# A cheaper VectorE exponential, a shorter rsqrt chain and an earlier preparation of heads in an attention kernel with normalized queries and keys

## Chip, cores and metric

One core of one Trainium2 chip. The metric is the device time of one execution in microseconds (us), the median of the runs. All runs quoted are of the state "fast". Engines: PE is TensorE (PEld its weight loads), DVE is VectorE, ACT is ScalarE, POOL is GpSimd, SP (SPq its queue) is SyncE, which here does nothing but issue DMAs, in a fixed order. In the views of the profile L402 is line 402 of that kernel, `p_ring<-psA` means that `psA` is read and `p_ring` written, and "issue" stands for idle time for which the profile shows no cause.

## The reference

32 heads, 2048 tokens, 20 numbers per head and token (B=1). Each query and key is divided by its norm, the logits are scaled by one `t` per head, softmax, then the product with V:

```python
qn = q / (jnp.sqrt((q * q).sum(axis=-1, keepdims=True)) + eps)
kn = k / (jnp.sqrt((k * k).sum(axis=-1, keepdims=True)) + eps)
logits = jnp.einsum('bhqd,bhkd->bhqk', qn, kn) * t[None, :, None, None]
attn = _softmax(logits, axis=-1)
return jnp.einsum('bhqk,bhkd->bhqd', attn, v)
```

With heads of only 20, the matrix products are small. The 32 x 2048 x 2048 exponentials are the work, and they are shared between two engines.

## The kernel before

A small scheduler in the kernel takes all tasks with planned durations and priorities ("due", in units of heads) and fixes, once, the order in which each engine does them. Every engine then runs its list in order and waits for semaphores. **An engine can thus be held up by the head of its list although a later task could run.**

The keys of a head are 16 chunks of 128, and one chunk is four units of 512 queries. ScalarE takes most chunks: TensorE writes QK products into `psA`, ScalarE takes the exponential of three units at a time into `p_ring`, TensorE multiplies that with V into `psO`. VectorE takes 3, 3, 3, 4 chunks of four successive heads, with an exponential made of integer operations: a 16-bit integer that is linear in the logit is, read as fp16, roughly 2 to that power, and two products with its mantissa correct the error.

```python
DVE_TILES = [4 if h % 4 == 3 else 3 for h in range(H)]
[...]
# one VectorE chunk: four evictions (t1), two integer passes (r, m), two fp16 products (T, U)
t1 = ... eng.tensor_scalar(xt[s][:, 512*g:512*g+512], psD[:, :], X_MUL, X_ADD, ALU.mult, ALU.add)
tr_ = ... eng.tensor_single_scalar(rr[s], xt[s], 0x3FF, ALU.bitwise_xor)
tm  = ... eng.tensor_scalar(mm[s2], xt[s], 0x3FF, 0x3C00, ALU.bitwise_and, ALU.bitwise_or)
tT  = ... eng.tensor_tensor(tt[s2], xt[s].bitcast(FP16), mm[s2].bitcast(FP16), ALU.mult)
tU  = ... eng.tensor_tensor(uu[s], tt[s2], mm[s2].bitcast(FP16), ALU.mult)
# the exponential is the sum of three terms, made by three products with V, two of them on scaled V
pS = pv("S", xt[s], v8, t1s); pR = pv("R", rr[s], v2, [tr_]); pU = pv("U", uu[s], vaug, [tU])
```

(shortened). Before its first QK product a head must be prepared:

```python
def add_prep(h):
    due = h - 1.6                    # planned 1.6 heads before the head is due
    # SyncE: loads of q (4), k, v
    # VectorE: squares, sums, 11 small steps of a reciprocal square root, normalize into qkn
    # SyncE: one transpose qkT<-qkn, four copies qz<-qkT, six copies kR<-qkT
```

The first QK product of a head waits for the last of those ten copies. `psD` is a single PSUM bank in which the QK products of VectorE's chunks go by, one unit at a time.

## Time and profile before

859.52 us (two runs, 858.82 and 860.21). The page of the profiled execution, its first part (busy time and share of the span):

```profile
span 855.5 us, 12498 instructions
## 1 busy us (share of the span) xinstructions
PE 706.3 (83%) x4836; PEld 201.5 (24%) x4928; DVE 783.2 (92%) x1380; ACT 749.7 (88%) x546; POOL 52.9 (6%) x79
```

No engine is alone at its limit. The groups of instructions (busy us, mean ns of one | idle time of the engine just before them, and what ended it):

```profile
L402 ACT ACTIVATE p_ring<-psA 128x1536 bf16<-128x1536 f32 x544 | 748.2, 1463 | 100.4 <-PE psA L342 84.2 <-remote 6.0 <-PE psO L351 4.4
...
L430 DVE TENSOR_SCALAR xt<-psD 128x512 int16<-128x512 f32 x416 | 284.1, 683 | 55.2 <-PE psD L342 50.1 <-remote 1.1 <-PE psO L351 1.0
...
L443 DVE TENSOR_TENSOR uu<-tt,mm 128x2048 f16<-128x2048 f16 x104 | 126.6, 1217 | 0.0
...
L437 DVE TENSOR_SCALAR mm<-xt 128x2048 int16<-128x2048 int16 x104 | 71.3, 685 | 0.0
```

ScalarE did nothing for 100.4 us of the span. Some 28 us of this is the start, as the list of waits shows (total us, times, longest):

```profile
ACT p_ring L402 <- PE psA L342: 84.2, 68, 28.3
...
DVE xt L430 <- PE psD L342: 50.1, 56, 6.4
PE psA L342 <- DMA kR<-qkT: 45.5, 8, 29.4
...
PE psD L342 <- DMA kR<-qkT: 10.1, 6, 3.0
```

To find what the rest is, take its longest stop, at 571 us. ScalarE's timeline (start, duration, and in brackets the idle time before):

```profile
560.96 1.45 ACT L402 ACTIVATE p_ring<-psA 128x1536 bf16<-128x1536 f32 x1 [0.21 <-PE psA L342]
570.63 2.79 ACT L402 ACTIVATE p_ring<-psA 128x1536 bf16<-128x1536 f32 x2 [8.22 <-PE psA L342]
574.61 1.45 ACT L402 ACTIVATE p_ring<-psA 128x1536 bf16<-128x1536 f32 x1 [1.19 <-PE psD L342]
576.78 1.45 ACT L402 ACTIVATE p_ring<-psA 128x1536 bf16<-128x1536 f32 x1 [0.72 <-PE psA L342]
```

The same stop in TensorE's timeline. It had waited for a kR copy:

```profile
569.45 0.60 PE L342 MATMUL psA<-qz,kR 64*128 64x512 bf16 x1 [4.64 <-DMA kR<-qkT]
...
569.99 1.69 PE L342 MATMUL psA<-qz,kR 128*128 128x512 bf16 x4
571.47 0.63 PE L342 MATMUL psD<-qz,kR 128*128 128x512 bf16 x1
```

And in SyncE's, the copies of that head, issued behind a transpose, which itself came when the head had been normalized, at 556.8:

```profile
556.84 1.27 SPq L315 DMA_TRANSPOSE qkT<-qkn  x1
558.15 2.69 SPq L268 DMA_DIRECT2D qk_sb<-in_q_dram  x4
560.89 0.62 SPq L271 DMA_DIRECT2D qk_sb<-in_k_dram  x1
561.57 2.48 SPq L321 DMA_DIRECT2D qz<-qkT  x4
564.09 3.77 SPq L327 DMA_DIRECT2D kR<-qkT  x6
```

Ten copies at 0.6 us each and the loads of another head lie between transpose and first product; with 2.1 us for the last copy to land, that makes 569.4, when TensorE goes on. This is a **late head**. ScalarE's gaps after the stop are 1.19 and 0.72 us, not the usual 0.2. The slices of the page (clock granted to TensorE, tenths of full speed, 40 slices):

```profile
PEclk9999999999999999899997999979999899999799
```

Busy time by stretches of 100 us (busy us and count per engine; then the granted clock):

```profile
core 0: us, PE busy (x) PEld busy (x) DVE busy (x) ACT busy (x) POOL busy (x), PEclk, DMA share, GB/s
500.00:600.00 100.00, 81.79 (x541) 22.77 (x550) 89.88 (x162) 84.13 (x62) 7.11 (x8) 0.91 0.24 40
700.00:800.00 100.00, 87.19 (x621) 25.15 (x632) 97.69 (x173) 94.89 (x71) 5.19 (x6) 0.99 0.21 40
```

### The profile page before, as it was taken

Reading aid. Unit: us, or ns where it says so; the run is one execution under the profiler, and the core shown is the slowest. Engines: PE = TensorE matmul, PEld = TensorE weight load, DVE = VectorE, ACT = ScalarE, POOL = GpSimd, SP = SyncE. Lnnn points to the kernel's source line nnn. Section 1 sums busy time; section 2 is a strip of 40 time slices with the busy share of each in tenths; the row PEclk is TensorE's granted clock in tenths of the full one; section 3 lists DMA queues with packets and bytes.
Section 4 is the critical chain, followed back from the end, with each engine's and each line's share of the span. In section 5 each row is a group of like instructions: output and inputs, shape, how many; then the busy total and the mean of one; then the engine's idle time right before and its main releaser. Section 6 shows DMA issues by size and latency. Waiting matters only on the chain.

```text
span 855.5 us, 12498 instructions
## 1 busy us (share of the span) xinstructions
PE 706.3 (83%) x4836; PEld 201.5 (24%) x4928; DVE 783.2 (92%) x1380; ACT 749.7 (88%) x546; POOL 52.9 (6%) x79
## 2 busy tenths in 40 slices
PE   0598998989887988788986998959988798898887
PEld 0122222222222222122221222212222122222122
DVE  7699998989998999799987999879998899999798
ACT  0599999989999899799986999859998799999797
POOL 3000000001000000000000101000000000000000
PEclk9999999999999999899997999979999899999799
DMA  6441203331213330413314213042121421220200
GB/s 54 89 65 30 49 10 53 53 52 23 47 38 54 53 53 5 67 35 53 47 14 67 54 32 53 8 77 44 31 44 18 80 34 37 45 41 22 66 1 8
DMA packets 198346, 36.49 MB, mean 43 GB/s; under 512 B 173712, under 2 KB 198288, under 8 KB 198288
## 3 DMA queue, kind: packets, MB, share of 16 engines
q1 hardware_dynamic: 198288, 35.70, 25.4%
q8 instruction: 38, 0.62, 0.3%
q14 instruction: 20, 0.16, 0.1%
HBM read 7.87 MB, written 2.62 MB: 12 GB/s over the span
## 4 chain that ended last, share of the span: by engine, by line
DVE 51%; PE 26%; SPq 13%; DMA 4%; issue 3%; ACT 2%
DVE xt L430 19%; PE psA L342 12%; DVE tt L440 9%; PE psO L351 8%; DVE uu L443 8%; PE psD L342 6%; SPq L327 5%; SPq L321 4%; DVE mm L437 3%; SPq L268 3%; DMA kR<-qkT 3%; DVE rr L435 3%; ACT p_ring L402 2%; DVE qkn L310 2%; DVE oT L360 2%
## 5 line engine op out<-in xcount | busy, mean ns | idle before, releaser
L402 ACT ACTIVATE p_ring<-psA 128x1536 bf16<-128x1536 f32 x544 | 748.2, 1463 | 100.4 <-PE psA L342 84.2
L342 PE MATMUL psA<-qz,kR 64*128 64x512 bf16 (+1 forms) x1169 | 316.1, 401 | 61.5 <-DMA kR<-qkT 43.7
L430 DVE TENSOR_SCALAR xt<-psD 128x512 int16<-128x512 f32 x416 | 284.1, 683 | 55.2 <-PE psD L342 50.1
L351 PE MATMUL psO<-p_ring,vaug 128*32 128x512 bf16 x1632 | 165.6, 396 | 8.4 <-issue 5.3
L342 PEld LDWEIGHTS psA<-qz,kR 64*128 64x128 bf16 (+1 forms) x1224 | 85.1, 94 | 267.9 <-issue 163.7
L342 PE MATMUL psD<-qz,kR 128*128 128x512 bf16 x296 | 119.2, 403 | 34.4 <-DVE xt L430 15.7
L342 PE MATMUL psA<-qz,qkT 64*128 64x512 bf16 (+1 forms) x395 | 133.3, 400 | 5.3 <-DMA kR<-qkT 1.8
L443 DVE TENSOR_TENSOR uu<-tt,mm 128x2048 f16<-128x2048 f16 x104 | 126.6, 1217 | 0.0
L440 DVE TENSOR_TENSOR tt<-xt,mm 128x2048 f16<-128x2048 f16 x104 | 126.5, 1216 | 0.1
L435 DVE TENSOR_SCALAR rr<-xt 128x2048 int16<-128x2048 int16 x104 | 71.4, 686 | 0.2
L437 DVE TENSOR_SCALAR mm<-xt 128x2048 int16<-128x2048 int16 x104 | 71.3, 685 | 0.0
L351 PEld LDWEIGHTS psO<-p_ring,vaug 128*32 128x32 bf16 x1632 | 42.0, 93 | 110.7 <-issue 100.9
L279 POOL TENSOR_SCALAR v<-vaug 128x128 bf16<-128x128 bf16 x32 | 21.7, 677 | 701.8 <-DMA vaug<-in_v_dram 701.8
L351 PE MATMUL psO<-uu,vaug 128*32 128x512 f16 x416 | 41.8, 392 | 19.8 <-DVE uu L443 18.7
L342 PEld LDWEIGHTS psD<-qz,kR 128*128 128x128 bf16 x312 | 30.3, 97 | 96.3 <-DVE xt L430 57.7
L342 PEld LDWEIGHTS psA<-qz,qkT 64*128 64x128 bf16 (+1 forms) x408 | 32.6, 94 | 68.6 <-issue 51.7
L351 PE MATMUL psO<-xt,v 128*32 128x512 f16 x416 | 41.4, 388 | 8.1 <-DVE oT L360 5.8
L342 PE MATMUL psD<-qz,qkT 128*128 128x512 bf16 x96 | 38.4, 400 | 6.5 <-DVE xt L430 4.7
L351 PE MATMUL psO<-rr,v 128*32 128x512 f16 x416 | 41.2, 386 | 1.5 <-DVE rr L435 1.1
L286 DVE TENSOR_TENSOR sq<-qk_sb 128x640 f32<-128x640 bf16 x32 | 26.2, 819 | 3.4 <-DMA qk_sb<-in_k_dram 3.2
L280 POOL TENSOR_SCALAR v<-vaug 128x128 bf16<-128x128 bf16 x32 | 27.4, 856 | 2.0
L360 DVE STREAM_TRANSPOSE oT<-psO 128x512 f32<-128x512 f32 x32 | 22.7, 710 | 5.2 <-PE psO L351 4.9
(29 smaller groups left out, 190.9 us busy)
## 6 DMA issues: line engine op xcount, KB each, us to landing
kR<-qkT SPq DMA_DIRECT2D x64, 96.0 KB, 2.1
qz<-qkT SPq DMA_DIRECT2D x128, 32.0 KB, 1.9
kR<-qkT SPq DMA_DIRECT2D x64, 64.0 KB, 2.0
qk_sb<-in_q_dram SPq DMA_DIRECT2D x128, 20.0 KB, 2.5
qk_sb<-in_k_dram SPq DMA_DIRECT2D x32, 80.0 KB, 2.5
vaug<-in_v_dram SPq DMA_DIRECT2D x32, 80.0 KB, 3.2
out_dram<-o_stage SPq DMA_DIRECT2D x32, 80.0 KB, 1.9
kR<-qkT SPq DMA_DIRECT2D x64, 32.0 KB, 1.9
```

The source lines that it names most:

```text
L280: return eng.tensor_scalar(v8[b][:, :, :], vaug[b][:, R - VD:R, :], 8.0, None, ALU.mult)
L321: rot[h].append(add("SP", f"qz{h}", lambda eng, tk, g=g: eng.dma_start(qz[bt][32 * g:32 * g + 32, g, :], qkT[bt][32 * g:32 * g + 32, 0:512 ...
L327: rot[h].append(add("SP", f"rot{h}", lambda eng, tk, d0=d0, s0=s0, m=m, dl=dl: eng.dma_start(kR[bt][d0:d0 + m, dl - 1, :], qkT[bt][s0:s0 + ...
L342: return eng.matmul(dst, lhsT, qz[bt][ps, g, :], tile_position=(p0, 0))
L351: last = eng.matmul(psO[32 * g:32 * g + 32, :], lhsT, rhs_of(g), start=start, stop=False, skip_group_check=True, tile_position=(0, 32 * g))
L360: tr = add("DVE", f"tr{h}", lambda eng, tk: eng.transpose(oT[:, :, :].rearrange("p r d -> p (r d)"), psO[:, :]), 0.62, pv_users[h] + ([fin ...
L402: act[w] = add("ACT", f"exp{w}", lambda eng, tk: eng.activation(p_ring[:, p0 * 512:p0 * 512 + n], psA[:, slot * WAVE * 512:slot * WAVE * 5 ...
L430: t1 = add("DVE", f"t1.{j}.{g}", lambda eng, tk, g=g: eng.tensor_scalar(xt[s][:, 512 * g:512 * g + 512], psD[:, :], X_MUL, X_ADD, ALU.mult ...
L435: tr_ = add("DVE", f"r{j}", lambda eng, tk: eng.tensor_single_scalar(rr[s][:, :], xt[s][:, :], 0x3FF, ALU.bitwise_xor), 0.60, t1s + old.ge ...
L437: tm = add("DVE", f"m{j}", lambda eng, tk: eng.tensor_scalar(mm[s2][:, :], xt[s][:, :], 0x3FF, 0x3C00, ALU.bitwise_and, ALU.bitwise_or), 0.60,
L440: tT = add("DVE", f"T{j}", lambda eng, tk: eng.tensor_tensor(tt[s2][:, :], xt[s][:, :].bitcast(FP16), mm[s2][:, :].bitcast(FP16), ALU.mult ...
L443: tU = add("DVE", f"U{j}", lambda eng, tk: eng.tensor_tensor(uu[s][:, :], tt[s2][:, :], mm[s2][:, :].bitcast(FP16), ALU.mult), 1.13, [tT] ...
```

## The change

The intent: less VectorE work per chunk (one fp16 product in place of two, three integer passes in place of two; all three terms on unscaled V, so GpSimd's scaling of V goes), more chunks for VectorE (3, 4, 3, 4: 112 of 512 in place of 104), a shorter rsqrt chain, and heads prepared earlier. The core of the diff, cuts marked:

```diff
-KEXP = 12.9958
+KEXP = 0.63116
+KE_BITS = 6
+SHIFT = 288
 [...]
-X_ADD = 1024.0 * (15.0 - math.log2(KEXP))
+X_ADD = 1024.0 * (15.0 + math.log2(KEXP))
 [...]
-        allt = sorted(self.tasks, key=lambda t: (t.start, t.seq))
+        allt = sorted(self.tasks, key=lambda t: (t.start, pos[t.seq]))
 [...]
-    DVE_TILES = [4 if h % 4 == 3 else 3 for h in range(H)]
+    DVE_TILES = [4 if h % 2 else 3 for h in range(H)]
 [...]
-            due = h - 1.6
+            due = h - 2.2
 [...]
-            vsc[h] = add("POOL", f"vsc{h}", vscale, 0.8, [ld_v[h]] + z_v[b], due)
 [...]
-            c.append(dv("rs", lambda eng, tk: eng.tensor_single_scalar(
-                rs["u"][:, :].bitcast(I32), rs["sum"][:, :].bitcast(I32), 1, ALU.logical_shift_right), 0.12, [c[-1]]))
             c.append(dv("rs", lambda eng, tk: eng.tensor_scalar(
-                rs["u"][:, :].bitcast(I32), rs["u"][:, :].bitcast(I32), 1597463007, -1, ALU.subtract, ALU.mult),
+                rs["u"][:, :].bitcast(I32), rs["sum"][:, :].bitcast(I32), -0.5, 1597463007.0, ALU.mult, ALU.add),
 [...]  (two Newton steps; the first of their instructions, a = y * y, stays)
-                c.append(dv("rs", lambda eng, tk: eng.tensor_tensor(
-                    rs["b"][:, :], rs["a"][:, :], rs["sum"][:, :], ALU.mult), 0.12, [c[-1]]))
-                c.append(dv("rs", lambda eng, tk: eng.tensor_scalar(
-                    rs["c"][:, :], rs["b"][:, :], -0.5, 1.5, ALU.mult, ALU.add), 0.12, [c[-1]]))
-                [...]
-                    tgt[:, :], cur[:, :], rs["c"][:, :], ALU.mult), 0.12, [c[-1]]))
+                c.append(dv("rs", lambda eng, tk: eng.scalar_tensor_tensor(
+                    rs["b"][:, :], rs["a"][:, :], -0.5, rs["sum"][:, :], ALU.mult, ALU.mult), 0.12, [c[-1]]))
+                c.append(dv("rs", lambda eng, tk, cur=cur, tgt=tgt: eng.scalar_tensor_tensor(
+                    tgt[:, :], rs["b"][:, :], 1.5, cur[:, :], ALU.add, ALU.mult), 0.12, [c[-1]]))
 [...]
-            qk = add("PE", f"qkA{w}", f_qk, 0.22 * (len(us) - 1), deps, due_a(us[0]) - 100)
+            qk = add("PE", f"qkA{w}", f_qk, 0.22 * max(1, len(us) - 1), deps, due_a(us[0]) - 100)
 [...]
-                rr[s][:, :], xt[s][:, :], 0x3FF, ALU.bitwise_xor), 0.60, t1s + old.get("r", []), due)
+                ee[s][:, :], xt[s][:, :], 0x7C00, KE_BITS, ALU.bitwise_and, ALU.bitwise_or), 0.60,
+                t1s + old.get("e", []), due)
+            t5 = add(SH_ENG, f"s{j}", lambda eng, tk: eng.tensor_scalar(
+                ss[s][:, :], xt[s][:, :], float(SHIFT - 4096), None, ALU.add), SH_DUR, t1s + old.get("s", []), due)
 [...]
-                mm[s2][:, :], xt[s][:, :], 0x3FF, 0x3C00, ALU.bitwise_and, ALU.bitwise_or), 0.60,
+                mm[s2][:, :], xt[s][:, :], 0x3FF, 0x3800, ALU.bitwise_and, ALU.bitwise_or), 0.60,
 [...]
-            tU = add("DVE", f"U{j}", lambda eng, tk: eng.tensor_tensor(
-                uu[s][:, :], tt[s2][:, :], mm[s2][:, :].bitcast(FP16), ALU.mult), 1.13,
-                [tT] + old.get("u", []), due)
 [...]
-            pS = pv("S", xt[s], v8[b][:, rv, :], t1s)
-            pR = pv("R", rr[s], v2[b][:, rv, :], [tr_])
-            pU = pv("U", uu[s], vaug[b][:, r, :], [tU])
+            pE, pS, pT = pv("E", ee[s], te), pv("S", ss[s], t5), pv("T", tt[s], tT)
```

The chain has 8 steps in place of 11. The two small lines (sort key, `max(1, ...)`) are there for correctness: with 112 chunks ScalarE's units no longer divide by three, the last wave has one unit and a planned duration of zero. A build of the kernel before with only the new chunk counts was found by the race check to let TensorE write a bank of `psA` that ScalarE still read; it was never run.

More of the change, by code (lines that the diff above doesn't have):

```diff
@@ L176, in bass_standalone__qk_norm__prompt_kernel @@
     NX = 3
-    DVE_TILES = [4 if h % 4 == 3 else 3 for h in range(H)]
+    DVE_TILES = [4 if h % 2 else 3 for h in range(H)]
     PE_GROUP = 0.27
-    VD = 4
+    SH_ENG, SH_DUR = "DVE", 0.60
     with ExitStack() as es:
@@ L188, in bass_standalone__qk_norm__prompt_kernel @@
         vaug = [sbuf(f"vaug{i}", [128, R, 32], BF16) for i in range(NB)]
-        v2 = [sbuf(f"v2{i}", [128, VD, 32], BF16) for i in range(NB)]
-        v8 = [sbuf(f"v8{i}", [128, VD, 32], BF16) for i in range(NB)]
         sq = sbuf("sq", [128, 2 * R, D], F32)
-        rs = {x: sbuf(f"rs_{x}", [128, 2 * R], F32) for x in ("sum", "u", "a", "b", "c", "y", "r")}
+        rs = {x: sbuf(f"rs_{x}", [128, 2 * R], F32) for x in ("sum", "u", "a", "b", "y", "r")}
         qkn = [sbuf(f"qkn{i}", [128, 2 * R, 32], BF16) for i in range(2)]
@@ L198, in bass_standalone__qk_norm__prompt_kernel @@
         xt = [sbuf(f"xt{i}", [128, 2048], I16) for i in range(NX)]
-        rr = [sbuf(f"rr{i}", [128, 2048], I16) for i in range(NX)]
+        ee = [sbuf(f"ee{i}", [128, 2048], I16) for i in range(NX)]
+        ss = [sbuf(f"ss{i}", [128, 2048], I16) for i in range(NX)]
         mm = [sbuf(f"mm{i}", [128, 2048], I16) for i in range(2)]
-        tt = [sbuf(f"tt{i}", [128, 2048], FP16) for i in range(2)]
-        uu = [sbuf(f"uu{i}", [128, 2048], FP16) for i in range(NX)]
+        tt = [sbuf(f"tt{i}", [128, 2048], FP16) for i in range(NX)]
         oT = sbuf("oT", [128, R, 32], F32)
@@ L246, in due_a @@
             return h + (i - a0[h]) / nA_head[h]
-        ld_qk, ld_v, norm, trn, rot, vsc = {}, {}, {}, {}, {}, {}
+        ld_v, norm, trn, rot = {}, {}, {}, {}
         qk_users = {h: [] for h in range(H)}
         pv_users = {h: [] for h in range(H)}
-        vs_users = {h: [] for h in range(H)}
         def bc(ap2d, n):
@@ L273, in add_prep @@
             src_v = v[0, h].rearrange("(p r) d -> p r d", p=128)
-            warv = (pv_users[h - NB] + vs_users[h - NB] + [vsc[h - NB]]) if h >= NB else z_v[b]
+            warv = pv_users[h - NB] if h >= NB else z_v[b]
             ld_v[h] = add("SP", f"ldv{h}", lambda eng, tk: eng.dma_start(vaug[b][:, :, 0:D], src_v),
                           0.6, warv, due - 0.4, lat=3.0, dma=f"v{b}")
-            def vscale(eng, tk):
-                eng.tensor_scalar(v2[b][:, :, :], vaug[b][:, R - VD:R, :], 2.0, None, ALU.mult)
-                return eng.tensor_scalar(v8[b][:, :, :], vaug[b][:, R - VD:R, :], 8.0, None, ALU.mult)
-            vsc[h] = add("POOL", f"vsc{h}", vscale, 0.8, [ld_v[h]] + z_v[b], due)
             def dv(name, fn, dur, deps):
@@ L289, in add_prep @@
                         0.75, [c[-1]]))
-            c.append(dv("rs", lambda eng, tk: eng.tensor_single_scalar(
-                rs["u"][:, :].bitcast(I32), rs["sum"][:, :].bitcast(I32), 1, ALU.logical_shift_right), 0.12, [c[-1]]))
             c.append(dv("rs", lambda eng, tk: eng.tensor_scalar(
-                rs["u"][:, :].bitcast(I32), rs["u"][:, :].bitcast(I32), 1597463007, -1, ALU.subtract, ALU.mult),
+                rs["u"][:, :].bitcast(I32), rs["sum"][:, :].bitcast(I32), -0.5, 1597463007.0, ALU.mult, ALU.add),
                 0.12, [c[-1]]))
             cur = rs["u"]
-            for it in range(2):
+            for tgt in (rs["y"], rs["r"]):
                 c.append(dv("rs", lambda eng, tk, cur=cur: eng.tensor_tensor(
                     rs["a"][:, :], cur[:, :], cur[:, :], ALU.mult), 0.12, [c[-1]]))
-                c.append(dv("rs", lambda eng, tk: eng.tensor_tensor(
-                    rs["b"][:, :], rs["a"][:, :], rs["sum"][:, :], ALU.mult), 0.12, [c[-1]]))
-                c.append(dv("rs", lambda eng, tk: eng.tensor_scalar(
-                    rs["c"][:, :], rs["b"][:, :], -0.5, 1.5, ALU.mult, ALU.add), 0.12, [c[-1]]))
-                tgt = rs["r"] if it == 1 else rs["y"]
-                c.append(dv("rs", lambda eng, tk, cur=cur, tgt=tgt: eng.tensor_tensor(
-                    tgt[:, :], cur[:, :], rs["c"][:, :], ALU.mult), 0.12, [c[-1]]))
-                cur = rs["y"]
+                c.append(dv("rs", lambda eng, tk: eng.scalar_tensor_tensor(
+                    rs["b"][:, :], rs["a"][:, :], -0.5, rs["sum"][:, :], ALU.mult, ALU.mult), 0.12, [c[-1]]))
+                c.append(dv("rs", lambda eng, tk, cur=cur, tgt=tgt: eng.scalar_tensor_tensor(
+                    tgt[:, :], rs["b"][:, :], 1.5, cur[:, :], ALU.add, ALU.mult), 0.12, [c[-1]]))
+                cur = tgt
             c.append(dv("rs", lambda eng, tk: eng.tensor_scalar(
@@ L434, in add_dtile @@
                 t1s.append(t1)
-            tr_ = add("DVE", f"r{j}", lambda eng, tk: eng.tensor_single_scalar(
-                rr[s][:, :], xt[s][:, :], 0x3FF, ALU.bitwise_xor), 0.60, t1s + old.get("r", []), due)
+            te = add("DVE", f"e{j}", lambda eng, tk: eng.tensor_scalar(
+                ee[s][:, :], xt[s][:, :], 0x7C00, KE_BITS, ALU.bitwise_and, ALU.bitwise_or), 0.60,
+                t1s + old.get("e", []), due)
+            t5 = add(SH_ENG, f"s{j}", lambda eng, tk: eng.tensor_scalar(
+                ss[s][:, :], xt[s][:, :], float(SHIFT - 4096), None, ALU.add), SH_DUR, t1s + old.get("s", []), due)
@@ L437, in add_dtile @@
             tm = add("DVE", f"m{j}", lambda eng, tk: eng.tensor_scalar(
-                mm[s2][:, :], xt[s][:, :], 0x3FF, 0x3C00, ALU.bitwise_and, ALU.bitwise_or), 0.60,
+                mm[s2][:, :], xt[s][:, :], 0x3FF, 0x3800, ALU.bitwise_and, ALU.bitwise_or), 0.60,
                 t1s + old2.get("m", []), due)
             tT = add("DVE", f"T{j}", lambda eng, tk: eng.tensor_tensor(
-                tt[s2][:, :], xt[s][:, :].bitcast(FP16), mm[s2][:, :].bitcast(FP16), ALU.mult), 1.13,
-                [tm] + old2.get("t", []), due)
@@ L443, in add_dtile @@
-            tU = add("DVE", f"U{j}", lambda eng, tk: eng.tensor_tensor(
-                uu[s][:, :], tt[s2][:, :], mm[s2][:, :].bitcast(FP16), ALU.mult), 1.13,
-                [tT] + old.get("u", []), due)
-            b = h % NB
-            rv = r - (R - VD)
-            base = [vsc[h]] + ([trO[h - 1]] if h else [])
-            def pv(nm, tile, wt, deps):
+                tt[s][:, :], xt[s][:, :].bitcast(FP16), mm[s2][:, :].bitcast(FP16), ALU.mult), 1.13,
+                [tm] + old.get("t", []), due)
@@ L451, in pv @@
+            wt = vaug[h % NB][:, r, :]
+            base = [ld_v[h]] + z_v[h % NB] + ([trO[h - 1]] if h else [])
+            def pv(nm, tile, dep):
                 p = add("PE", f"pv{nm}{j}", lambda eng, tk: pv_mm(
-                    eng, h, wt, lambda g: tile[:, 512 * g:512 * g + 512].bitcast(FP16)), PE_GROUP, deps + base, due + 0.2)
+                    eng, h, wt, lambda g: tile[:, 512 * g:512 * g + 512].bitcast(FP16)), PE_GROUP, [dep] + base,
+                    due + 0.2)
                 pv_users[h].append(p)
@@ L454, in pv @@
                 return p
-            pS = pv("S", xt[s], v8[b][:, rv, :], t1s)
-            pR = pv("R", rr[s], v2[b][:, rv, :], [tr_])
-            pU = pv("U", uu[s], vaug[b][:, r, :], [tU])
-            vs_users[h] += [pS, pR, pU]
-            x_users[j] = {"x": [tr_, tm, tT, pS], "r": [pR], "m": [tT, tU], "t": [tU], "u": [pU]}
+            pE, pS, pT = pv("E", ee[s], te), pv("S", ss[s], t5), pv("T", tt[s], tT)
+            x_users[j] = {"x": [te, t5, tm, tT], "e": [pE], "s": [pS], "m": [tT], "t": [pT]}
```

## The prediction

> **What bounds it now.** Page, part 1: VectorE is busy 783.2 us (92%), ScalarE 749.7 (88%), TensorE 706.3 (83%) of 855.5. No engine alone is the limit: after a start of 30 us (the first exponential starts at 30.6), VectorE and ScalarE are both about 93% busy by windows, and stop together when a head is late. In the list of waits ScalarE waits 84 us for QK products, 28.3 of it the start; the rest is some 15 stops of 1 to 8 us (279, 358, 462, 571, 676 us ...) with slow restarts, and many gaps of 0.2 to 0.4. In the chain of waits these stops end with kR<-qkT DMAs and the SyncE queue (13% of the chain, start included). At 571 us: the rsqrt links of that load lay scattered between large VectorE instructions, it was normalized at 556, and transpose plus 15 DMA issues of 0.6 us brought it at 569.4, too late. From 700 to 800 us, where almost no head is late, VectorE is 97.7% and ScalarE 94.9% busy, with 71 exponential instructions and 14 VectorE chunks, against 62 and 12 from 500 to 600.
>
> **What the change does** (start-to-start times in the timeline, as neighbours overlap).
> - VectorE chunk: four evictions (0.60), two integer passes (0.60), two products (1.13) = 5.9 us; after: four, three, one = 5.3. The Trainium skill ("VectorE: DVE Perf Modes", the perf-mode tier table) gives tensor_scalar on 16-bit SBUF data four results a cycle, tensor_tensor two; the durations of 686 and 1217 ns here agree. The new int16 add should cost 0.60 too. Chunks 104 to 112: 610 to 597 us.
> - rsqrt chain 11 links to 8, each 0.1 us interleaved, 0.22 back to back: -10 us of work; and 3 to 5 us sooner per head, where one link is done per 1 to 2 us. VectorE in all: about 760.
> - ScalarE: 544 to 534 instructions of 1.375 us: 735.
> - TensorE: 8 more VectorE chunks, about +10 us.
> - GpSimd's scaling of V (49 us) goes; it was off the path.
> - Normalization 0.6 head (15 us) sooner: the longest stop is 8 us, so nearly all late heads should vanish. This is the largest part: of 72 us of ScalarE waiting after the start, about 45 belong to such stops.
> - 3,4,3,4 chunks leave VectorE and ScalarE near 23 to 24 us per head on average.
>
> **Sum.** 859.5 - 14 (ScalarE work) - 35 to 45 (stops) = 800 to 810. Cross-check (estimate): 30 start + 735/0.95 + 4 end = 808. TensorE, 716 us of work, was at most 90.6% busy (30 to 100 us); at that rate 825. I predict 810 us, range 793 to 834. Chances: faster by over 2% 0.94, within 2% 0.05, slower 0.01.
>
> **To check after.** VectorE busy 750 to 770 us, ScalarE 735, its waits for QK 45 to 60 instead of 84; TensorE's waits for kR beyond the start below 5 (now 16); the int16 add 0.68 to 0.69 us; stops of several us gone; first exponential 1 to 2 us sooner.
>
> **What would make it wrong.** The int16 add at two a cycle (+0.5 us x 112); the earlier preparation held up by in-order SyncE waits (stores wait 112 us there) or buffers, so that heads are still late (then 835 to 845); TensorE becoming the limit, since three 0.6 us passes give a QK round trip through the single psD bank less cover than two and two 1.13 us products did.

## The result

783.2 us (782.79 and 783.62), ratio 0.9112, 95% interval 0.9073 to 0.9151. A ratio here and below is the mean time of one kernel's fast runs over that of the kernel before in the same rounds, so it is not quite the ratio of the medians. The direction was right; the time lies below the range of 793 to 834.

The page after, first part:

```profile
span 781.0 us, 12650 instructions
## 1 busy us (share of the span) xinstructions
PE 716.0 (92%) x4992; PEld 202.2 (26%) x4992; DVE 750.5 (96%) x1348; ACT 734.1 (94%) x536; POOL 3.8 (0%) x15
```

Groups of instructions:

```profile
L392 ACT ACTIVATE p_ring<-psA 128x1536 bf16<-128x1536 f32 x534 | 732.6, 1458 | 42.0 <-PE psA L332 35.5
...
L420 DVE TENSOR_SCALAR xt<-psD 128x512 int16<-128x512 f32 x448 | 307.0, 685 | 11.7 <-PE psD L332 8.4
...
L433 DVE TENSOR_TENSOR tt<-xt,mm 128x2048 f16<-128x2048 f16 x112 | 136.3, 1217 | 0.0
...
L428 DVE TENSOR_SCALAR ss<-xt 128x2048 int16<-128x2048 int16 x112 | 76.8, 686 | 0.0
```

List of waits; of the 35.5 us, 27.2 are the start, and no kR wait but the first is left:

```profile
ACT p_ring L392 <- PE psA L332: 35.5, 26, 27.2
PE psA L332 <- DMA kR<-qkT: 28.3, 1, 28.3
...
DVE xt L420 <- PE psD L332: 8.4, 27, 0.9
```

Granted clock in slices, and one stretch:

```profile
PEclk9999999999999999999999999999999999999999
```

```profile
core 0: us, PE busy (x) PEld busy (x) DVE busy (x) ACT busy (x) POOL busy (x), PEclk, DMA share, GB/s
500.00:600.00 100.00, 96.39 (x669) 27.46 (x669) 99.05 (x179) 98.50 (x73) 0.00 (x0) 1.00 0.30 48
```

VectorE and ScalarE are now both at 98 to 99%, and TensorE at 96%. Two neighbours in TensorE's timeline, to compare with the 0.6 us matmuls after the stop above; they last 0.4 us:

```profile
560.08 0.40 PE L341 MATMUL psO<-p_ring,vaug 128*32 128x512 bf16 x4
560.41 0.39 PE L332 MATMUL psD<-qz,kR 128*128 128x512 bf16 x1
```

**Where the time came from.** ScalarE's record can be summed without a rest: time to its first exponential, busy time of the exponentials, waiting between them, time from its last exponential to the end (worked out from the two traces, us):

```
          to the first   busy   waiting (in gaps >= 1 us)   to the end    sum
before        30.6      748.2      72.1  (48.1)                4.7        855.6
after         29.5      732.6      14.8  ( 2.5)                4.1        781.0
difference    -1.1      -15.6     -57.3                       -0.6        -74.6
```

Three quarters of the gain are waiting that is gone; the exponentials that moved to VectorE are a fifth.

Two more quantities from the traces, used for all runs below. *Late heads*: of heads 4 to 31, those for whose first QK product TensorE's list came to the wait for the head's last kR copy before that copy had landed, or less than 0.3 us after (landings as the trace assigns them). Before: 16 of 28, after: 0 of 28, with 4.6 to 28.5 us to spare (median 8.4). From normalization to landing it is 14 us in both. Of the 48.1 us of stops before, 47.0 lie between 6 us before and 12 us after the landing of a late head, which is 35% of the time. *Half clock*: time between ScalarE's first and last exponential in which TensorE's granted clock was 0.5. Before: 64.9 us, in ten stretches, each a multiple of 3.4 us, each beside a TensorE gap of 1.4 to 4.6 us; after: none. (Two such gaps, at 189 and 244 us, brought no half clock.) Of ScalarE's 72.1 us of waiting before, 31.8 lie inside those stretches, 8.7 of them while TensorE stood still anyway.

### The profile page after: what moved, and what is told of

It reads as the page before. It is cut to its first block, busy times and chain, and to the rows that moved or that the text cites. A ratio compares the mean times of both kernels' runs of the same rounds, so it can differ in the third digit from the quotient of the medians.

```text
span 781.0 us, 12650 instructions
## 1 busy us (share of the span) xinstructions
PE 716.0 (92%) x4992; PEld 202.2 (26%) x4992; DVE 750.5 (96%) x1348; ACT 734.1 (94%) x536; POOL 3.8 (0%) x15
## 4 chain that ended last, share of the span: by engine, by line
DVE 60%; PE 26%; SPq 5%; issue 4%; ACT 4%; DMA 1%; ACTq 0%; DVEq 0%
DVE xt L420 24%; DVE tt L433 12%; PE psA L332 11%; PE psO L341 9%; PE psD L332 6%; DVE mm L430 5%; DVE ee L425 5%; DVE ss L428 4%; ACT p_ring L392 4%; DVE sq L281 2%; DVE qkn L300 2%; SPq L268 2%; DVE rs_sum L283 2%; SPq L317 2%; DVE oT L350 1%
## 5 line engine op out<-in xcount | busy, mean ns | idle before, releaser
L392 ACT ACTIVATE p_ring<-psA 128x1536 bf16<-128x1536 f32 x534 | 732.6, 1458 | 42.0 <-PE psA L332 35.5
L420 DVE TENSOR_SCALAR xt<-psD 128x512 int16<-128x512 f32 x448 | 307.0, 685 | 11.7 <-PE psD L332 8.4
L332 PE MATMUL psD<-qz,kR 128*128 128x512 bf16 x336 | 130.5, 388 | 14.0 <-DVE xt L420 10.4
L433 DVE TENSOR_TENSOR tt<-xt,mm 128x2048 f16<-128x2048 f16 x112 | 136.3, 1217 | 0.0
L425 DVE TENSOR_SCALAR ee<-xt 128x2048 int16<-128x2048 int16 x112 | 76.8, 686 | 0.1
L428 DVE TENSOR_SCALAR ss<-xt 128x2048 int16<-128x2048 int16 x112 | 76.8, 686 | 0.0
L341 PE MATMUL psO<-ee,vaug 128*32 128x512 f16 x448 | 44.5, 387 | 4.3 <-DVE ee L425 3.7
L332 PEld LDWEIGHTS psA<-qz,qkT 64*128 64x128 bf16 (+1 forms) x400 | 31.8, 94 | 63.5 <-issue 51.1
L341 PE MATMUL psO<-tt,vaug 128*32 128x512 f16 x448 | 44.4, 386 | 4.0 <-DVE tt L433 2.2
L341 PE MATMUL psO<-ss,vaug 128*32 128x512 f16 x448 | 44.5, 387 | 1.3 <-DVE ss L428 0.6
L300 DVE TENSOR_TENSOR qkn<-qk_sb,rs_r 128x640 bf16<-128x640 bf16 x32 | 26.1, 815 | 4.3 <-DMA qkT<-qkn 4.1
L283 DVE TENSOR_REDUCE rs_sum<-sq 128x32 f32<-128x640 f32 x32 | 25.8, 805 | 0.1
L350 DVE STREAM_TRANSPOSE oT<-psO 128x512 f32<-128x512 f32 x32 | 22.7, 710 | 1.6 <-PE psO L341 1.4
```

The costliest lines, as they stand in the source:

```text
L283: c.append(dv("sum", lambda eng, tk: eng.tensor_reduce(rs["sum"][:, :], sq[:, :, :], AXIS_X, ALU.add), 0.75, [c[-1]]))
L300: norm[h] = dv("norm", lambda eng, tk: eng.tensor_tensor(qkn[b2][:, :, 0:D], x[:, :, :], bc(rs["r"][:, :], 2 * R), ALU.mult), 0.75, [c[-1] ...
L332: return eng.matmul(dst, lhsT, qz[bt][ps, g, :], tile_position=(p0, 0))
L341: last = eng.matmul(psO[32 * g:32 * g + 32, :], lhsT, rhs_of(g), start=start, stop=False, skip_group_check=True, tile_position=(0, 32 * g))
L350: tr = add("DVE", f"tr{h}", lambda eng, tk: eng.transpose(oT[:, :, :].rearrange("p r d -> p (r d)"), psO[:, :]), 0.62, pv_users[h] + ([fin ...
L392: act[w] = add("ACT", f"exp{w}", lambda eng, tk: eng.activation(p_ring[:, p0 * 512:p0 * 512 + n], psA[:, slot * WAVE * 512:slot * WAVE * 5 ...
```

## The experiments

**Theory L:** the earlier preparation ends the late heads, and all of ScalarE's waiting, small gaps too, was their aftermath. **Rival X:** the small gaps come from TensorE's in-order list waiting for the second fp16 product, so the new exponential removes them. A third question is what the short chain is worth. All kernels below gave correct results. In these rounds the kernel before ran at 856.7 to 857.8 us (medians). All runs in one table (time; ratio and interval; ScalarE's waiting; half clock; late heads):

```
                              us     ratio [95%]              waiting  half   late
before                      859.5                                72.1  64.9    16
before + lead 2.2           816.0  0.9523 [0.9482, 0.9564]       30.7   6.8    13
before + short chain        829.2  0.9684 [0.9652, 0.9716]       46.0  27.3    15
before + lead + chain       796.3  0.9296 [0.9263, 0.9330]       14.7   0      5
before + exponential        822.6  0.9605 [0.9563, 0.9646]       36.8  10.2    16
after, old exponential      863.9  1.0076 [1.0045, 1.0106]       81.2  17.1    0
after, lead 1.6             825.6  0.9621 [0.9572, 0.9670]       47.3  27.3    12
after, lead 1.9             808.6  0.9435 [0.9393, 0.9477]       37.8  23.9    18
after, long chain           794.1  0.9271 [0.9249, 0.9294]       18.8   0      0
after, 3,3,3,4 chunks       802.8  0.9380 [0.9351, 0.9408]       20.5   0      13
  the same, four buffers    801.4  0.9349 [0.9330, 0.9369]       21.5   6.8    1
after, loads held back      786.2  0.9180 [0.9159, 0.9202]       16.5   0      0
after                       783.2  0.9112 [0.9073, 0.9151]       14.8   0      0
after, loads from ScalarE   774.9  0.9042 [0.9024, 0.9061]       11.3   0      0
```

The number of late heads does not say how late they are. TensorE's idle time that ends with a late head's landing does: 30.7 us before, 8.6 with the lead alone, 21.2 with the chain alone, none with both, 16.8 with the exponential alone; in the kernel after, 22.0 with lead 1.6, 19.2 with 1.9, none with 2.2. In these runs ScalarE's waiting falls in the same order. ("After, old exponential" waits 81.2 us with no late head, for another reason; see there.)

### The lead alone

```diff
-            due = h - 1.6
+            due = h - 2.2
```
(in the kernel before)

> The kernel before with one line changed: heads are prepared 2.2 ahead in place of 1.6 (long rsqrt chain, old exponential, 26 of 32 head pairs unchanged). Theory L (the lead alone removes the late heads, and the small ScalarE gaps of 0.2 to 0.4 us were their aftermath): ScalarE's waits for QK after the start fall from 56 us to under 15, VectorE is over 97% busy between 100 and 700 us, the time is set by VectorE's 783 us of work: 803 to 815 us. Theory X (the small gaps come from the in-order TensorE queue waiting for the second fp16 product, 33 us in the weight loads and 19 us in the matmuls): only the stops of over 1 us go, small gaps stay, VectorE 94 to 95%: 820 to 830 us.

815.98 us. The list of waits:

```profile
ACT p_ring L402 <- PE psA L342: 54.4, 62, 28.6
```

One line of the change gives 41 us, more than half of the gain. Stops of 1 us or more fall from 48.1 to 8.0 us, half clock from 64.9 to 6.8. But 25.8 us of QK waits after the start (54.4 - 28.6) are neither L's 15 nor X's picture: the time sits on the edge between both. The late heads explain it: 13 of 28 are still late, by less. Their small waits do not show as kR waits; the list puts many of them down to a VectorE instruction or to "issue" that ended at about the same time. Only the comparison of landing and first use shows them.

### Lead and short chain, and the chain alone

The rsqrt part of the diff, with the lead and without it, old exponential and chunks:

> The kernel before with lead 2.2 and the short rsqrt chain, old exponential and 3,3,3,4 chunks. Theory L: the chain counts only as VectorE work, about 32 x 3 x 0.1 = 10 us less than the lead alone: 793 to 805 us. If instead the chain's length decides whether heads are late, this run is over 20 us faster than the lead alone.

796.30 us: 19.7 below the lead alone. VectorE's work fell by 10.6 us (773.3 to 762.7 busy), and ScalarE's waiting by 16.0 (30.7 to 14.7), with 5 late heads in place of 13. So the chain counts both as work and as lateness. The two are not separate sums, since less VectorE work also makes heads ready sooner. This kernel waits no more than the kernel after, with the old exponential in it:

```profile
ACT p_ring L397 <- PE psA L337: 36.3, 38, 27.2
```

This decides against X: gaps under 1 us are down to 13.5 us (12.3 in the kernel after), while TensorE's weight loads still wait 30.3 us for the second product (`uu`; 32.9 before) and its matmuls 10.6 (18.7). And with the new exponential alone (below) these gaps stay at 25.0 us (23.9 before). L was too strong as well: 12.3 us of small gaps stay in the kernel after, where no head is late.

> The kernel before with the short chain alone, lead 1.6. Landing 3 to 5 us sooner covers part of the late heads (16 of 28 late in the kernel before): 825 to 845 us. If only its 10.6 us of VectorE work counts, at 93% busy it hides in waits: 846 to 857.

829.18 us, as expected of a chain that acts through late heads: alone it gives 27.5 us (of 856.7), of which 10.6 us can be work. As many as 15 heads are still late, but by less. Alone the two parts give 41 and 27 us, together 60 and not 68: in part they cure the same thing.

### The exponential alone

The kernel after with lead 1.6, the long chain and 3,3,3,4 chunks:

> Only the new exponential (no scaling of V): long rsqrt chain, lead 1.6, 3,3,3,4 chunks as before. VectorE has 104 x 0.55 = 57 us less work than before. Theory L: heads are as late as before, so most of those 57 us turn into waiting: 835 to 860 us, ScalarE's QK waits after the start still over 40 us. Theory X: the gaps go with the second product: 800 to 820 us.

822.58 us, between the two forecasts; neither holds. With 52 us less of VectorE's work (783.2 to 731.5) heads are still late, 16 of 28, but by less, so half clock is 10.2 us and waiting halves to 36.8. VectorE had more idle time than before (the trace has 72.3 us of it after the first eviction, 57.6 before the change): the lighter exponential could not be used in full while preparation set the pace.

### The change with its lead put back, and half way

```diff
-            due = h - 2.2
+            due = h - 1.6        (second kernel: h - 1.9)
```
(in the kernel after)

> The kernel after with its lead put back to 1.6, all else as after. Theory L: the stops return, ScalarE waits for QK of 20 to 55 us after the start, TensorE waits for kR, 815 to 840 us. Theory X: the new exponential with its shorter dependency chain holds the gain, under 800 us.

825.61 us (its runs spread from 819 to 826; the profiled one was the fastest). The kR waits are back; the list:

```profile
ACT p_ring L392 <- PE psA L332: 59.6, 41, 27.0
...
PE psA L332 <- DMA kR<-qkT: 40.1, 6, 28.0
...
PE psD L332 <- DMA kR<-qkT: 7.2, 4, 2.1
```

> The kernel after with a lead of 1.9, midway between 1.6 (825.6 us) and 2.2 (783.2). A head takes 23.5 us, so 0.3 of it is 7 us; in the kernel after, the last copy of a head lands 4.6 to 12 us before its first use (median 8.4), so with 7 us less about a third of the heads should be late, each by under 3 us: ScalarE waits 20 to 35 us after the start (14.8 with 2.2, 47 with 1.6), 790 to 805 us. If the lead acts otherwise than by lateness, as by the order of VectorE's instructions, there is no reason for a time between the two.

808.60 us: between, as lateness has it, but worse than forecast (waiting 37.8 us, forecast 20 to 35; 18 of 28 heads late, forecast a third). More heads are late than with lead 1.6 (12), but TensorE's idle time for them is less (19.2 us, 22.0). The steps from 1.6 to 1.9 to 2.2 give 17 and 25 us. VectorE's work after its first eviction is 732.6 us here and 732.0 in the kernel after; only waiting differs.

### The change with the long chain

> The kernel after with the long rsqrt chain. Three more links per head are 10.6 us of VectorE work (762.7 against 773.3 in the two runs that differ so). In the kernel after, a head's last copy lands 4.6 to 12 us before its first use, so 3 to 5 us of later landing should leave nearly all on time: 792 to 797 us, all of it work. If the chain's length acts through late heads, as the 20 us between the two earlier runs suggest, over 800 us with ScalarE QK waits over 15 us after the start.

794.09 us, as forecast. No head is late (least margin 0.9 us), the loss of 11 us is VectorE's 10.9 us of work (761.4 for 750.5 busy). Where the lead suffices, the chain is worth its work and no more.

### The change with the old exponential

Kernel before with lead 2.2, short chain, 3,4,3,4 chunks and the two small lines:

> Everything of the change except the exponential: lead 2.2, short chain, 3,4,3,4 chunks, with the old exponential of two products. VectorE has 762.7 + 8 x 5.9 = 810 us of work, so it bounds: 30 + (810 - 18) / 0.985 + 4 = 838 us (830 to 845), heads not late. Then moving eight chunks to VectorE is only worth it with the cheaper exponential, and the exponential's own part of the gain is the 13 us between 796.3 and 783.2. If ScalarE rather than VectorE bounds, it is under 800.

863.85 us, slower than the kernel before, and 26 us over the forecast. VectorE's work was as forecast (811.8 busy), no head is late, but VectorE sat idle for 32.5 us after its first eviction, where I had allowed 12, and ScalarE's waits have a new name:

```profile
ACT p_ring L397 <- PE psO L346: 60.7, 32, 5.9
...
DVE xt L425 <- PE psD L337: 28.0, 71, 1.2
```

ScalarE waits for places in `p_ring`, which are free only when the V products are done, and those wait in TensorE's list behind VectorE's chunks. While that list stands, VectorE's next QK product is not made either. An engine that is behind its plan holds up the one that feeds it. This reading is from the waits; I did not test it further. What the run does show: moving eight chunks to VectorE pays only with the cheaper exponential.

### The change with 3,3,3,4 chunks, three buffers and four

```diff
-    DVE_TILES = [4 if h % 2 else 3 for h in range(H)]
+    DVE_TILES = [4 if h % 4 == 3 else 3 for h in range(H)]
-    NT = 3
+    NT = 4               (second kernel only)
```

> The kernel after with 3,3,3,4 chunks per head (104 in place of 112). VectorE has 8 x 5.3 = 42 us less work (about 708), ScalarE 15 us more (748). If work decides where heads are on time, ScalarE bounds: 29.5 start + 748 / 0.985 + 4 = 793 us, so the new exponential without moving chunks is worth next to nothing against the lead and the short chain with the old exponential (796.3). If instead the uneven 3,3,3,4 pattern makes heads late (in the two runs with lead 2.2 and 3,3,3,4 the late heads came two of every four), late heads return and it is over 800 us.

802.75 us, the number that was forecast for an uneven pattern that makes heads late. VectorE has time to spare (68.5 us idle), ScalarE is busy for 744.7 us, and 13 heads are late again. From normalization to landing it took 34 us. My theory was that the transposes waited for buffers and that this cost the time. SyncE's own waits:

```profile
SPq L305 <- PE psA L332: 91.6, 13, 15.5
```

> The kernel after with 3,3,3,4 chunks (as the earlier run of 802.75 us) and four in place of three buffers for the transposed heads (qkT, qz, kR). In that earlier run VectorE had time to spare, so its chunks ran ahead of ScalarE, and each head's transpose waited until the QK products of three heads before had been done (SyncE waits of 92 us for psA, 34 us from normalization to landing in place of 14). If those buffers made the heads late, a fourth removes it: ScalarE waits for QK after the start under 12 us in place of 18, 790 to 796 us. If the uneven pattern itself does it, the time stays within 3 us of 802.75.

801.41 us, so the theory fell as to the time. With four buffers one head is late, normalization to landing is 15.5 us, and the time is the same. ScalarE's 21.5 us of waiting, mostly in gaps under 1 us, stay; what makes them stays open. Late heads are harmless here: with 13 of them ScalarE waits 20.5 us, with one 21.5. ScalarE sets the pace: 29.8 + 744.1 + 21.5 + 4.1 = 799.5 us. Against lead and chain with the old exponential (796.3) the new exponential gains nothing until chunks move.

### A shorter start

After the change the start is 29.5 of 781 us, and the first transpose stands in SyncE's list behind the loads of head 2 (issued at 14.1, although head 0 was normalized at 10.7).

First try: the loads of heads 2 and 3 wait for a normalization.

```diff
-            war = [norm[h - NB]] if h >= NB else []
+            war = [norm[h - NB]] if h >= NB else ([norm[h - 1]] if h >= 2 else [])
```

> The kernel after, but the loads of heads 2 and 3 wait for the normalization of heads 1 and 2, so the SyncE queue issues the first transpose and its ten copies right after the normalization in place of behind loads. The first exponential should start at about 24.5 to 25.5 in place of 29.5 us; everything behind it shifts with it: 778 to 780 us. If heads 1 to 3 become late by it, no gain.

786.23 us, 3 us slower. The first exponential comes 2 us sooner (27.5), but VectorE now idles for 13.3 us in one piece:

```profile
ACT p_ring L392 <- PE psA L332: 36.1, 41, 25.3
...
DVE xt L420 <- PE psD L332: 25.3, 41, 13.3
```

It did 11.0 us of work before its first eviction in place of 18.5, and the rest came later, when VectorE sets the pace. In this kernel, work that the bounding engine does in the start is free.

Second try: the loads of heads 1 to 3 are issued from ScalarE's queue.

```diff
+            le, lx, lp = ("ACT", "a", 20) if 1 <= h < NB else ("SP", "", 0)
-            lds.append(add("SP", f"ldq{h}", ... due - 0.5, lat=2.5, dma=f"q{b}"))
+            lds.append(add(le, f"ldq{h}", ... due - 0.5 - lp, lat=2.5, dma=f"q{lx}{b}"))
[...]   (the same for k and v)
```

The Trainium skill ("Trainium Kernel Development and Optimization", Key Constraints) says that DMAs of all queues run on the same 16 engines, and that issuing from several only saves the sequencer's issue time. That time, 0.6 us per issue in SyncE's timeline, is just what was short; that the engines are the same, no run here tests.

> The kernel after, with the first loads of heads 1 to 3 issued from ScalarE's queue, idle then, in place of SyncE's. SyncE is then free to issue the transpose of head 0 right after its normalization (10.7 us) and its ten copies right after that. First exponential at 23 to 25 us in place of 29.5. Unlike the earlier attempt, VectorE gets heads 1 to 3 early, so no VectorE work moves behind the start (its idle time before the first eviction should fall from 12 to about 6 us). Expected 776 to 780 us. If VectorE again has to do preparation later, 783 or more.

774.92 us (774.72 to 775.31), a little below the forecast: the fastest kernel, and its interval (0.9024 to 0.9061) lies below that of the kernel after. The first exponential starts at 25.0 us; VectorE did 18.4 us of work before its first eviction at 26.5, so it idled for 8.1 us there (forecast 6). The start gives 4.5 us; another 3.5 come from less waiting of ScalarE later on (14.8 to 11.3), which I had not forecast. SyncE's timeline in the start:

```profile
11.02 1.45 SPq L306 DMA_TRANSPOSE qkT<-qkn  x1
...
15.95 2.48 SPq L312 DMA_DIRECT2D qz<-qkT  x4
18.47 3.78 SPq L318 DMA_DIRECT2D kR<-qkT  x6
```

## Why the prediction was wrong

Right, point by point. VectorE's work: forecast about 760, range 750 to 770; 750.5 measured. ScalarE: 735; 734.1. TensorE: 716; 716.0. The integer add: 686 ns, at four results a cycle, as the perf-mode tier table of the Trainium skill ("VectorE: DVE Perf Modes") has it for tensor_scalar on bf16 data in SBUF; this trace agrees for int16. First exponential 1 to 2 us sooner: 1.1. kR waits beyond the start below 5 us: none. The cause of the waits, late heads, and their cure: shown by the runs with lead 1.6, 1.9 and 2.2, and by where the stops lie.

Wrong is one term of the sum: "35 to 45 (stops)" of "72 us of ScalarE waiting after the start", with 27 to 37 us of it left standing. Measured: 57.3 us went, 14.8 stayed. The stops of 1 us or more gave 45.6 us (48.1 to 2.5), the top of the forecast. The small gaps, 23.9 us, which the sum left standing as if they were a fixed cost, fell to 12.3. So the step that failed is to take only the stops as the late heads' cost. One of the points to check failed with it: ScalarE's waits for QK were to be 45 to 60 us, and are 35.5. With the measured terms the sum is 859.5 - 15.6 - 57.3 - 1.1 - 0.6 = 784.9, against 783.2.

Two readings led to it.

- "From 700 to 800 us, where almost no head is late" was false. By landing and first use three heads (28, 29 and 30) waited there, at 748.9, 770.8 and 798.4 us. I took 94.9% of ScalarE as the best that this kernel can do and built "735/0.95" on it. Without late heads it is 98 to 99%. The trace of the kernel before could have told: from 700 to 745 us, ahead of the first of the three, ScalarE is busy for 44.28 of 45 us (98.4%) and VectorE for 44.65. In the same way I took TensorE's 90.6% as a limit; it ran at 96% afterwards.
- The "slow restarts" were seen, and not followed. After most of its stops TensorE's clock is halved for 3.4 us or a multiple of it, and matmuls take 0.6 us in place of 0.4. The Trainium skill ("TensorE: Matmul & The Clock Gate", Part 1) describes the half clock after an idle window of about 3.4 us; the trace agrees in the factor and in the length of the stretches. In the kernel before these stretches hold 31.8 of the 72.1 us of waiting, but only 5.1 of the 23.9 us of small gaps. With the lead alone half clock fell to 6.8 us and the small gaps stayed at 22.7; they fell to 13.5 when lead and chain together left TensorE no idle time for a late landing. The runs fit a late head that costs its own wait and an aftermath in small gaps, of which the clock can be less than half (5.1 of 11.6 us). How much the clock costs by itself was not separated: no run varied the clock without the waits.

What each part is worth depends on the order. Taken as lead, then chain, then exponential with the new chunks, medians go 856.7, 816.0, 796.3, 783.2: 41, 20 and 13 us. The last step is ScalarE's lighter load (745.9 to 732.6 busy, 13.3 us) and nothing else in ScalarE's account: waiting is 14.7 and 14.8. In this order the headline of the change, the exponential, is its smallest part, and it needs the moved chunks to count; taken alone on the kernel before it gives 34 us, along with heads that are less late (TensorE's idle time for them is 16.8 us, not 30.7). Taken out of the finished change, with the chunks left where they are, it is worth 81 us (863.85 against 783.2).

Still open: what makes the 11 to 17 us of small gaps that the kernels with at most five late heads keep (23.5 with the old exponential and 112 chunks), and the full cause of the 26 us by which the old exponential with 112 chunks missed its forecast.

## What to carry to other kernels

When two engines wait together, find the hand-over that is late by comparing the landing of the data with its first use for every item, not by the longest entries of the list of waits: waits of under a microsecond are put down to whatever ended beside them. Do not take the best stretch of a trace as the engine's limit until you have checked that the stretch is free of the very stalls that the change removes. Latency is bought with lead, and only then does cheaper work on the bounding engine count in full; in the start, keep the bounding engine supplied before shortening anything else.

## What the Trainium skill lacked or had wrong

- "TensorE: Matmul & The Clock Gate", Part 1: its table of states names an idle window of about 3.4 us for the fall to half clock; further on it says that short idle times between groups of matmuls can bring it about too, and gives no length for them. Here stretches at half clock began beside TensorE gaps of 1.4 to 1.8 us (at 149, 429, 644 and 798 us in the kernel before), none of them as long as a window, and with the lead alone one began at 646.5 us with no gap above 0.7 us in the 6 us before it. Gaps of 1.8 and 2.3 us, at 244 and 189 us in the kernel before, brought none.
- "VectorE: DVE Perf Modes", The DRAIN you can't avoid: the page says the next instruction does not start until the pipe is empty, and that one which is not held starts earlier. In these traces the earlier start is the rule: instructions of 686 ns start 0.60 us apart, of 1217 ns 1.13 apart; small ones of 0.19 us that depend on each other start 0.22 apart. A sum of durations overstates VectorE (872 us of durations for 783.2 busy in the kernel before).
- The same page, perf-mode tier table: it has no row for `scalar_tensor_tensor`. Here 128 x 32 fp32 took 169 to 184 ns, as `tensor_tensor` did (180 to 183 ns in the same kernel). So small an instruction does not show the tier.
- "TensorEngine Tiling (Array Packing)", Key Properties: it says that a change of the tiling mode drains TensorE, but gives no cost. In the kernel before, TensorE's neighbours of one shape started 0.21 to 0.23 us apart (V products, 705.9 and 706.1 us), neighbours of different shape 0.32 (706.1 and 706.4 us).
